# Moving row loads to the GpSimd DMA queue and cutting block stores into quarters in a serial backward chain

## The chip, the cores and the metric

The kernel runs on one core of one Trainium2 chip. The metric is the device time of one execution in microseconds (us). Times are medians of several executions. Of a kernel's stages only the backward chain is changed, so a second number is used throughout: **the chain time**, read from the trace as the time from the first to the last of the copies that close a step (`GT<-ps_sum`), 63 step intervals. Each chain time below is of a single profile, and differences below about 3 us are not read.

## The reference, cut to what matters

The output is `x` plus two branches on its layer norm, and the kernel computes it together with all gradients. The first branch is recurrent: 64 segments of 32 rows, each attending over itself and over 8 memory rows that the segment before produced.

```python
mem = mem0
for s in range(n_seg):                                   # 64 segments
    xs = x[:, s * seg_len:(s + 1) * seg_len, :]          # 32 rows of 512
    h = jnp.concatenate([mem, xs], axis=1)               # 8 memory rows + 32
    q, k, v = (jnp.einsum('btd,dhe->bhte', h, W) for W in (Wq, Wk, Wv))   # 32 heads of 128
    p = _softmax(jnp.where(mask, jnp.einsum('bhqe,bhke->bhqk', q, k) * scale, -1e9))
    o = jnp.einsum('bhte,hed->btd', jnp.einsum('bhqk,bhke->bhqe', p, v), Wo)
    mem = o[:, :M, :]                                    # read by the next segment
    outs.append(o[:, M:, :])
# second branch: out = relu(x @ w1 + b1) ** 2 @ w2 + b2
_out, _vjp = jax.vjp(_f, x, mem0, Wq, Wk, Wv, Wo, w1, b1, w2, b2)
```

(The `q, k, v` line and the softmax are shortened here.) Because a segment's memory gradient comes from the segment after it, the backward pass is a chain of 64 steps that cannot overlap.

## The kernel before

The backward chain takes its steps in blocks of four, 16 blocks. One list of names per step (`B_ORDER`) fixes the order in which operations are issued. A bare name is an operation of this step, `-` means that of the step before, `L.` one of the block before, and `L.` with `+` one of this block. Each engine executes its own instructions in that order.

```python
B_ORDER = (
    "... o1te ldq- ldn- L.qo ldk- vtr vg0 ... qeb0 ldp kg0 ... qp1 ldn ... ra L.G1 sm vc sF L.H1 sT HT",   # first step
    ...,
    "L.ra3 o0mm L.qst o0ev L.ldt+ ... s1 d11 vg0 ldk- vlb1 ... vtr L.gs+ vla1 ldq- ... vc vg1 ... qp0 L.vo+ "
    "qeb0 ... L.ldv+ kp1 ... qp1 L.ldk+ qeb1 qea1 ldp kg1 L.ko+ qg1 ra sm sF L.sT sT HT")               # last step
```

All DMAs are issued by the SP queue (`dma = nc.sync.dma_start`). Of each step these are the loads of P, qN, kN and kLs, and a DMA transpose into `vl`, which two GpSimd copies then turn into `vT`. A step's names of row loads, `vtr` and `vc` stand for those of the step that comes next. So `ldq-` and `ldk-`, and `ldn-` in two steps of four, load rows of the very step in which they are issued.

```python
def ldp():
    dma(tile_of("P", [P, KH, KW])[:], rows[:, 3 * GW:AC].rearrange("p (k n) -> p k n", k=KH))
o["ldq"] = lambda: dma(tile_of("qN", [P, GW])[:], rows[:, GW:2 * GW])
o["ldn"] = lambda: dma(tile_of("kN", [P, GW])[:], rows[:, 2 * GW:3 * GW])
o["ldk"] = lambda: dma(tile_of("kLs", [P, GW])[0:P - M * j, :], S_NL[b, M * j:P, 1, :])
def vtr():
    nc.sync.dma_start_transpose(tile_of("vl", [P, KH, HG, SEG])[:]..., rows[:, 0:GW])
def vc():
    vT = tile_of("vT", [P, KH, HG, L])
    nc.gpsimd.tensor_copy(vT[:, :, :, 0:SEG], C["vl"][:])
    nc.gpsimd.tensor_copy(vT[:, :, :, SEG:L], B_["vTL"][:, :, :, lc])
```

The gradients gv, gk and gq of a block's four steps are collected in three tiles and stored once a block, 1 MB each. Every partition's 8 KB is contiguous on both sides, so a store has 8 KB descriptors:

```python
for t, n in enumerate("qkv"):
    o[n + "o"] = lambda n=n, t=t: dma(S_GB[b, t], B_["g" + n][:].rearrange("p g k j r -> p g k (j r)"))
```

TensorE's part is made of small matmuls: `outer` (into `b_pp`, in the chain of waits below 32 instructions in some 0.3 us) and `gather` (into `ps_gR`, 16 in about 1 us).

Of the kernel before, what the change touches and what calls it, by code (L numbers as in the profile page):

```python
# [10 lines left out]
BF16 = mybir.dt.bfloat16  # L11
F32 = mybir.dt.float32
P = 128
# [13 lines left out]
def kernel(  # L27
# [27 lines left out]
    nc = tc.nc  # L55

    _, S, D = A_x.shape
    M = A_mem0.shape[1]
# [35 lines left out]
    out2flat = out_2.flatten_outer_dims()  # L94

    dma = nc.sync.dma_start

    const = ctx.enter_context(tc.tile_pool(name="const", bufs=1))
    dram = ctx.enter_context(tc.tile_pool(name="dram", bufs=1, space=bass.MemoryType.DRAM))
# [813 lines left out]
    with sb("ls", 3) as ls, sb("lo", 1) as lo_, psum("lpp", 1) as lpp, psum("lr", 4) as lr:  # L913
# [84 lines left out]


    B_ORDER = (  # L1000
        "o0mm o0ev xt- L.xt- o1mm o0fl vp0 L.lq o1ev o0te o1fl s0 vea0 veb0 o1te ldq- ldn- L.qo ldk- vtr vg0 "
        "vlb0 d10 vla0 vp1 d20 d30 s1 L.G0 veb1 L.H0 d11 vlb1 vla1 d40 vea1 d21 tu0 kp0 kea0 klb0 keb0 d31 vg1 "
        "d41 kla0 qp0 qea0 qeb0 ldp kg0 tu1 kp1 kea1 klb1 L.sx- keb1 kla1 qg0 qp1 ldn qea1 qeb1 L.ra0 kg1 qg1 "
        "ra L.G1 sm vc sF L.H1 sT HT",
        "L.ra1 o0mm ldk- o1mm o0ev vtr o0fl o0te vp0 veb0 xt- o1ev vlb0 vla0 L.ktr vea0 s0 o1fl vp1 o1te L.G2 "
        "d10 d20 veb1 s1 vlb1 d30 vg0 d40 vea1 tu0 ldq- vla1 kp0 vg1 d11 kea0 kla0 d21 klb0 keb0 d31 d41 L.vtr "
        "qp0 qeb0 ldp qea0 tu1 vc kg0 kp1 kea1 qg0 keb1 kla1 klb1 qp1 kg1 qeb1 qea1 qg1 L.H2 ra sm sF sT L.ra2 "
        "HT",
        "xt- o0mm o0ev o1mm o0fl o1ev ldn- ldq- ldk- vp0 o1fl o0te s0 vlb0 veb0 d10 vla0 vea0 d20 d30 o1te vp1 "
        "vg0 vlb1 vtr s1 L.G3 vc vla1 veb1 d40 vea1 tu0 L.vst d11 d21 kp0 klb0 kea0 keb0 kla0 d31 vg1 L.kst d41 "  # L1010
        "qp0 qeb0 qea0 tu1 kg0 kp1 kea1 keb1 qg0 kla1 klb1 qp1 L.qtr kg1 qeb1 qea1 qg1 ra L.H3 sm sF sT ldp ldn "
        "HT",
        "L.ra3 o0mm L.qst o0ev L.ldt+ o1mm xt- o0fl L.gl+ o1ev vp0 o1fl o0te vlb0 vea0 vla0 s0 veb0 o1te vp1 "
        "d10 d20 d30 veb1 s1 d11 vg0 ldk- vlb1 d40 tu0 vea1 vtr L.gs+ vla1 ldq- d21 L.sm kp0 klb0 vc vg1 keb0 "
        "d31 L.sF kea0 kla0 d41 qp0 L.vo+ qeb0 tu1 kg0 qea0 L.ldv+ kp1 qg0 keb1 kla1 klb1 kea1 qp1 L.ldk+ qeb1 "
        "qea1 ldp kg1 L.ko+ qg1 ra sm sF L.sT sT HT")
    ENGS = on_engines(
        "L.ra0 L.sF kea0 kea1 kla0 kla1 o0ev o1ev o1te qea0 qeb1 ra sF vea0 vea1 veb1 vla0 vla1 vlb1 "
        "xt",
# [1 line left out]
    with sb("bq", 1) as bq, sb("bs", 2) as bs, sb("bt", 1) as bt, psum("bpp", 1) as bpp, psum("br", 4) as br:  # L1021
# [11 lines left out]
        def block(b):  # L1033
            if b not in blk:
                shapes = {"gkL": (bs, [P, KH, HG, NL], BF16), "gvL": (bs, [P, KH, HG, NL], BF16),
                          "gqL": (bt, [P, KH, HG, NL], BF16), "PG": (bt, [P, 1, KH, KW], BF16), "GL": (bt, [P, 1, KH, KW], BF16),
                          "gOL": (bt, [P, GW], BF16), "qNL": (bt, [P, GW], BF16), "vTL": (bt, [P, KH, HG, NL], BF16),
                          "XT": (bs, [P, DC, SPB, SEG], F32), "R4": (bt, [P, D], F32), "F": (bt, [P, P], F32),
                          "gv": (bt, [P, HG, KH, SPB, SEG], BF16), "gk": (bt, [P, HG, KH, SPB, SEG], BF16),
                          "gq": (bt, [P, HG, KH, SPB, SEG], BF16)}  # L1040

                def make(n):
                    pool, shape, dt = shapes[n]
                    return pool.tile(shape, dt, name="b_" + n, tag=n)
                blk[b] = Tiles(make)
            return blk[b]

        def left(b):
            B_ = block(b)
            ps, st, o = {}, {}, {}  # L1050
            src = {"v": "gvL", "k": "gkL", "q": "gqL"}
            o["lq"] = lambda: dma(B_["gqL"][:], S_GQL[b])

            def following(f):

                return lambda: f(b - 1) if b > 0 else None
            for n, f in loads.items():
                o[n] = following(f)
            o["gs"] = lambda: dma(S_GM[:, :, b * P:(b + 1) * P], gts[b][:])
            for t, n in enumerate("qkv"):  # L1060
                o[n + "o"] = lambda n=n, t=t: dma(S_GB[b, t], B_["g" + n][:].rearrange("p g k j r -> p g k (j r)"))

            jobs = [(WT[t], src[n], k) for t, n in ((2, "v"), (1, "k"), (0, "q")) for k in range(KH)]
            for i in range(4):
                for x, nm in enumerate("GH"):
                    def G_(i=i, x=x):
                        if x == 0:
                            ps["R", i] = big("ps_RL")
                        for m, (W, n, k) in enumerate(jobs[6 * i + 3 * x:6 * i + 3 * x + 3]):
                            for g in range(HG):  # L1070
                                nc.tensor.matmul(ps["R", i][32 * g:32 * g + 32, :], lhsT=B_[n][:, k, g, :],  # L1071
                                                 rhs=W[:, g * KH + k, :], start=(x == 0 and m == 0),
                                                 stop=(x == 1 and m == 2), tile_position=(0, 32 * g))
                    o["%s%d" % (nm, i)] = G_
                if i == 0:
                    o["ra0"] = lambda: ENGS["L.ra0"](B_["R4"][:], ps["R", 0][:])
                else:
                    o["ra%d" % i] = lambda i=i: nc.vector.tensor_tensor(out=B_["R4"][:], in0=ps["R", i][:],
                                                                        in1=B_["R4"][:], op=ALU.add)
            sum_ops(o, big, lambda: B_["R4"], lambda: B_["F"], st, "L.")  # L1080
            o["xt"] = lambda: ENGS["L.xt"](B_["XT"][:, :, :, 0:M],
                                                st["sum"].rearrange("p c (j t) -> p c j t", j=SPB))

            for t, n in enumerate("qkv"):
                def nt(n=n):
                    st[n] = bs.tile([P, KH, P], BF16, name="gNat", tag="gNat")
                    nc.sync.dma_start_transpose(st[n][:], B_[src[n]][:].rearrange("p k g r -> p k (g r)"))
                o[n + "tr"] = nt
                o[n + "st"] = lambda n=n, t=t: dma(S_GL[b].rearrange("g r t c -> (g r) t c")[:, t, :],
                                                   st[n][:].rearrange("p k e -> p (k e)"))  # L1090

            o["sx"] = lambda: dma(S_XG[b], B_["XT"][:].rearrange("p c j r -> p c (j r)"))
            return o
# [8 lines left out]
                nc.gpsimd.memset(gts[b][:, :, P - SEG:P - SEG + M], 0.0)  # L1102

        def ldv(b):
            dma(block(b)["PG"][:, 0], S_PL[b])
            dma(block(b)["gOL"][:], S_GOL[b])

        def ldk(b):
            dma(block(b)["GL"][:, 0], S_GSL[b])
            dma(block(b)["qNL"][:], S_NL[b][:, 0, :])  # L1110

        def ldt(b):
            turned_rows(block(b)["vTL"][:], b, 2)
# [2 lines left out]
        def bwd(s):  # L1116
# [12 lines left out]
                return C[n]  # L1129

            def ldp():
                dma(tile_of("P", [P, KH, KW])[:], rows[:, 3 * GW:AC].rearrange("p (k n) -> p k n", k=KH))
            o["ldp"] = ldp
            o["ldq"] = lambda: dma(tile_of("qN", [P, GW])[:], rows[:, GW:2 * GW])
            o["ldn"] = lambda: dma(tile_of("kN", [P, GW])[:], rows[:, 2 * GW:3 * GW])
            o["ldk"] = lambda: dma(tile_of("kLs", [P, GW])[0:P - M * j, :], S_NL[b, M * j:P, 1, :])

            def vtr():

# [8 lines left out]
            for p in range(2):  # L1148
# [43 lines left out]
                for t, n in ((2, "v"), (1, "k"), (0, "q")):  # L1192
                    w = 32 if n == "q" else KW
                    for x, h in enumerate("ab"):
                        e = "%se%s%d" % (n, h, p)
                        o[e] = lambda n=n, p=p, w=w, x=x, e=e: ENGS[e](
                            B_["g" + n][:, 2 * x:2 * x + 2, HALF[p], j, :],
                            two_of(ps["x", n, p], x, w)[:, :, :, 0:SEG])
                        if n != "q":
                            e = "%sl%s%d" % (n, h, p)  # L1200
                            o[e] = lambda n=n, p=p, x=x, e=e: ENGS[e](
                                B_["g%sL" % n][:, HALF[p], 2 * x:2 * x + 2, lc].rearrange("p k g r -> p g k r"),
                                two_of(ps["x", n, p], x, KW)[:, :, :, SEG:L])

                    def G_(n=n, p=p, t=t):
                        if "R" not in ps:
                            ps["R"] = big("ps_gR")
                            ps["n"] = 0
                        ps["n"] += 1
                        gather(ps["R"], lambda k, g: B_["g" + n][:, g, k, j, :], WT[t], p, ps["n"] == 1,  # L1210
                               ps["n"] == 6)
                    o["%sg%d" % (n, p)] = G_
            def ra():
# [189 lines left out]
```

## Time and profile before

The time is 3290.86 us (2 executions, 3289.17 to 3292.55). The busy time of each engine in four stretches of the kernel before shows the stages. The columns are the stretch, its length, each engine's busy time with its instruction count, the granted TensorE clock, the busy share of the DMA engines and what they moved.

```profile
core 0: us, PE busy (x) PEld busy (x) DVE busy (x) ACT busy (x) POOL busy (x), PEclk, DMA share, GB/s
488.00:1425.00 937.00, 770.15 (x18868) 406.50 (x18868) 509.92 (x1588) 381.72 (x833) 51.54 (x128) 0.97 0.67 169
...
1602.00:2623.00 1021.00, 860.63 (x25194) 414.13 (x25195) 432.46 (x1338) 383.12 (x1181) 89.79 (x129) 0.96 0.68 176
2623.00:3266.00 643.00, 570.51 (x2682) 262.57 (x2733) 58.50 (x89) 74.81 (x161) 36.99 (x32) 0.95 0.97 192
```

The first row is the forward chain (recurrence forward), the second the backward chain with its start and end, the last the weight gradients. TensorE is busy 861 of 1021 us.

The steps of a block are not alike: on average 18.9, 14.1, 14.3 and 16.4 us from first to last. The middle two show what a step costs; the excess sits around a block's turn. What TensorE and then the SP queue waited for in the backward stretch of the kernel before (columns: who waited for whom, us in total, times, longest):

```profile
PE b_pp L563 <- issue: 45.8, 34, 4.7
PE ps_gR L478 <- issue: 20.8, 16, 2.8
PE ps_proj L437 <- DVE GT L424: 17.9, 63, 0.3
...
PE b_pp L563 <- DMA b_qN<-S_A: 12.3, 11, 2.7
```

```profile
SPq L1132 <- DVE gS L522: 215.1, 48, 9.8
SPq L1135 <- PE b_pp L563: 148.5, 49, 6.7
```

"Issue" means that the profile shows nothing that TensorE waited for. The wait for GT belongs to every step (0.3 us, 63 times). The wait for `b_qN` is a load that came late, and the two SP lines say why: SP stands in line, 215 us before the load of P and 149 us before that of kN, and what is behind cannot leave.

The chain of waits of the kernel before, around one block's last step (columns: start, length, what), has both kinds of gap:

```profile
2034.34 3.92 DMA b_qN<-S_A
...
2040.92 0.18 PE b_pp L563 x12
2041.10 2.77 issue
2043.88 0.32 PE b_pp L563 x12
```

First TensorE waits for a load that took 3.92 us. Then it stops for 2.77 us in the middle of a run of 32 matmuls, where the profile shows nothing that it waits for. The DMA records suggest why: an instruction fetch runs from 2041.37 to 2042.25 us, and TensorE resumes 1.6 us after it landed. In the queue part of the page of the kernel before, queue 8 holds these fetches (columns: packets, MB, share of the 16 engines' time):

```profile
q1 hardware_dynamic: 890418, 625.81, 77.0%
q8 instruction: 406, 6.65, 0.8%
```

6.65 MB in 406 fetches is 16 KB each; 192 of them fall in the chain, one per 256 instructions. I call a gap between matmuls of over 0.8 us a **fetch gap** when it ends 1.0 to 1.8 us after a fetch landed. The chain before has 34 of them, 66.1 us of its 74.7 us in gaps over 0.8 us. (The prediction counted a slightly longer window: 35, 68 us.) That they are stalls on the fetch is an inference from this timing.

### The profile page before, as it was taken

The numbers are of one execution on the slowest core, as the hardware profiler recorded it, in microseconds if no ns is written. First come the engines' busy times: TensorE is split into PE (matmuls) and PEld (weight loads), VectorE is DVE, ScalarE is ACT, GpSimd is POOL, SyncE is SP. The second block draws the span as 40 slices with busy tenths as digits, with TensorE's granted clock in tenths as the row PEclk, the third lists the DMA queues.
The fourth block names the chain that finished last, engine by engine and source line by source line (L and its number), as shares of the span: only waits on it lengthen the run. The fifth ranks groups of instructions, "written<-read, shape, count | busy, mean of one in ns | idle before, by whom it ended". The sixth has DMA issues, their size and how long they took to land.

```text
span 3266.8 us, 115469 instructions
## 1 busy us (share of the span) xinstructions
PE 2704.2 (83%) x51673; PEld 1338.9 (41%) x51768; DVE 1220.4 (37%) x3526; ACT 1017.1 (31%) x2492; POOL 193.7 (6%) x345
## 2 busy tenths in 40 slices
PE   8898778888888888834688888888888866999998
PEld 4453334444444444412344344344344423444444
DVE  4440035555655555523344344444444400010001
ACT  3331124444444444412333333333333401111111
POOL 0000000000000000000000010010000000000000
PEclk9999899999999999966799999999999988999999
DMA  9958894676667676689668666666776699999993
GB/s 254 283 145 312 293 291 114 165 179 162 185 164 184 161 184 161 171 235 256 185 164 210 166 164 181 189 164 172 190 183 172 173 260 199 205 186 224 187 187 91
DMA packets 890915, 633.20 MB, mean 194 GB/s; under 512 B 659745, under 2 KB 748466, under 8 KB 881074
## 3 DMA queue, kind: packets, MB, share of 16 engines
q1 hardware_dynamic: 890418, 625.81, 77.0%
q8 instruction: 406, 6.65, 0.8%
q14 instruction: 91, 0.75, 0.1%
HBM read 227.16 MB, written 250.10 MB: 146 GB/s over the span
## 4 chain that ended last, share of the span: by engine, by line
PE 57%; DMA 13%; SPq 13%; DVE 7%; issue 5%; ACT 5%; ACTq 0%; POOLq 0%; POOL 0%; DVEq 0%
PE ps_gR L478 11%; PE ps_proj L437 11%; PE ps_gw L1364 8%; SPq L1289 6%; PE b_pp L563 3%; PE ps_R L478 3%; DMA S_GOL<-l_gON 3%; PE ps_tr L167 2%; ACT R L421 2%; PE ps_sum L489 2%; PE ps_L L406 2%; DMA out_dram<-wt 2%; PE ps_w L366 2%; PE ps_w L386 1%; PE ps_RL L1071 1%
## 5 line engine op out<-in xcount | busy, mean ns | idle before, releaser
L1364 PE MATMUL ps_gw<-gn,HNc 128*128 128x512 bf16 x1881 | 416.5, 380 | 8.3 <-ACT wt L1339 6.3
L437 PE MATMUL ps_proj<-Wqkv,X 128*32 128x512 bf16 x6144 | 361.9, 385 | 18.2 <-DVE X L424 17.9
L1364 PEld LDWEIGHTS <-HNc 128*128 128x128 bf16 x1920 | 188.2, 98 | 231.9 <-issue 9.5
L421 ACT CAST f_N<-ps_proj 128x512 bf16<-128x512 f32 x320 | 185.4, 583 | 258.0 <-PE ps_proj L437 243.7
L1339 ACT CAST wt<-ps_gw 128x512 bf16<-128x512 f32 x126 | 69.5, 591 | 541.8 <-DMA out_dram<-wt 353.1
L437 PEld LDWEIGHTS <-X 128*32 128x32 bf16 x6144 | 156.9, 98 | 174.7 <-DVE X L424 29.9
L1322 DVE TENSOR_TENSOR gx<-ps_rows,gb 128x512 f32<-128x512 f32 x16 | 11.1, 692 | 427.5 <-PE ps_rows L1320 396.8
L1364 PE MATMUL ps_gw<-GOc,gn 128*128 128x512 bf16 x627 | 142.2, 387 | 19.2 <-DMA gn<-S_ON 18.3
L478 PE MATMUL ps_gR<-WT,b_gq 128*32 128x512 bf16 x2048 | 145.2, 401 | 7.8 <-issue 7.5
L478 PE MATMUL ps_gR<-WT,b_gk 128*32 128x512 bf16 x2048 | 145.8, 404 | 5.8 <-issue 5.7
L478 PE MATMUL ps_gR<-WT,b_gv 128*32 128x512 bf16 x2048 | 142.5, 393 | 7.6 <-issue 7.5
L437 PE MATMUL ps_proj<-WoT,GT 128*32 128x512 bf16 x2048 | 125.6, 388 | 22.5 <-DVE GT L424 17.9
L478 PE MATMUL ps_R<-Wo,OT 128*32 128x512 bf16 x2048 | 127.1, 390 | 0.0
L1145 POOL COPY b_vT<-b_vl 128x1024 bf16<-128x1024 bf16 x64 | 66.7, 1042 | 905.9 <-PE ps_sc L458 521.4
L421 ACT CAST gON<-ps_proj 128x512 bf16<-128x512 f32 x128 | 75.0, 586 | 118.9 <-PE ps_proj L437 115.2
L489 PE MATMUL ps_sum<-R,sel 128*32 128x128 f32 x1152 | 61.2, 285 | 58.4 <-ACT R L421 53.0
L1364 PEld LDWEIGHTS <-gn 128*128 128x128 bf16 x640 | 63.6, 100 | 96.4 <-DMA gn<-S_ON 18.6
L406 PE MATMUL ps_L<-Wqkv,XL 128*128 128x512 bf16 x376 | 84.8, 385 | 18.2 <-DMA XL<-S_XL 16.8
L421 ACT CAST b_gq<-b_pp 128x256 bf16<-128x256 f32 x128 | 47.7, 373 | 161.4 <-PE b_pp L563 153.3
L421 ACT CAST b_gk<-b_pp 128x256 bf16<-128x256 f32 x128 | 47.8, 373 | 150.7 <-PE b_pp L563 115.5
L424 DVE CAST b_gq<-b_pp 128x256 bf16<-128x256 f32 x128 | 54.4, 425 | 107.0 <-PE b_pp L563 102.8
L437 PEld LDWEIGHTS <-GT 128*32 128x32 bf16 x2048 | 49.5, 98 | 78.4 <-DVE GT L424 30.0
(214 smaller groups left out, 4427.9 us busy)
## 6 DMA issues: line engine op xcount, KB each, us to landing
S_A<-f_N SPq DMA_DIRECT2D x64, 512.0 KB
out_dram<-wt SPq DMA_DIRECT2D x154, 128.0 KB
S_A<-f_N SPq DMA_DIRECT2D x64, 256.0 KB
S_ON<-OC SPq DMA_DIRECT2D x64, 256.0 KB
b_qN<-S_A SPq DMA_DIRECT2D x64, 256.0 KB
b_kN<-S_A SPq DMA_DIRECT2D x64, 256.0 KB
S_GB<-b_gv SPq DMA_DIRECT2D x16, 1024.0 KB
S_GB<-b_gk SPq DMA_DIRECT2D x16, 1024.0 KB
```

What stands on the lines that cost most here:

```text
L167: nc.tensor.transpose(ps_ap, in_ap, ident[base:base + k, base:base + k])
L366: nc.tensor.matmul(ps[:], lhsT=aN[:, rc, fc * P:(fc + 1) * P], rhs=gN[:, rc, :], start=(rc == 0), stop=(rc == TC - 1))
L406: nc.tensor.matmul(ps[:], lhsT=XL[:, dc, q * P:(q + 1) * P], rhs=Wqkv[:, dc, c0:c0 + 512], start=(dc == 0), stop=(dc == DC - 1))
L421: nc.scalar.copy(out, in_)
L437: nc.tensor.matmul(ps[32 * g:32 * g + 32, :], lhsT=hT[:, dc, :], rhs=W[:, dc, c:c + 4 * P], start=(dc == 0), stop=(dc == DC - 1), tile_pos ...
L478: nc.tensor.matmul(R[32 * g:32 * g + 32, :], lhsT=XT(k, g), rhs=W[:, g * KH + k, :], start=(first and k == 4 * h), stop=(last and k == 4 * ...
L489: nc.tensor.matmul(ps["n"][SEG * c:SEG * c + SEG, 0:P], lhsT=sel[:], rhs=R4()[:, c * P:(c + 1) * P], start=True, stop=True, tile_position= ...
L563: nc.tensor.matmul(o, lhsT=N_[32 * g:32 * g + m, kk * P:(kk + 1) * P], rhs=X(kk)[32 * g:32 * g + m], start=(i == 0), stop=(i == len(jobs) ...
L1145: nc.gpsimd.tensor_copy(vT[:, :, :, 0:SEG], C["vl"][:])
L1289: nc.sync.dma_start_transpose(t_[:, b, :].rearrange("p (k e) -> p k e", k=KH), blocks(b)[:, g].rearrange("p k r -> p (k r)"))
L1339: nc.any.tensor_copy(wt[:], ps[:])
L1364: nc.tensor.matmul(ps[:], lhsT=l(rc), rhs=r(rc), start=(n == 0), stop=(n == RC_ALL - 1))
```

## The change

The intent: no load stands behind SP's waits, each arrives a step ahead, and stores are small and leave as soon as their data is there. It has three parts: row and block loads are issued by GpSimd, a step ahead; each 1 MB store becomes four of 256 KB, with 1 KB descriptors, each behind its copies; and the turned left values `vTL` get a second buffer (at the cost of one of `gNat`), so their transpose moves from the last step of the block before to its second step. `vtr` stands at the start of each step and `vc` behind the scores. (The transposes into `gNat` and their stores move a little too, all on SP.) The order of work on TensorE, VectorE and ScalarE stays.

```diff
+    pdma = nc.gpsimd.dma_start
     B_ORDER = (
-        "o0mm o0ev xt- ... ldq- ldn- L.qo ldk- vtr vg0 ... qeb0 ldp kg0 tu1 kp1 ... qp1 ldn ... ra L.G1 sm vc sF L.H1 sT HT",
+        "o0mm vtr o0ev xt- ... d30 s1 vc L.G0 ... d41 ldp kla0 ... kp1 ldq kea1 ... qp1 ldn ldk qea1 ... L.H1 sT HT",
   ... (second and third step alike)
-        "... L.ldt+ ... ldk- ... vtr ... ldq- ... vc vg1 ... qp0 L.vo+ ... L.ldv+ ... L.ldk+ ... ldp kg1 L.ko+ qg1 ..."
+        "... vtr ... vea0 L.voa0+ ... veb0 L.vob0+ o1te vp1 L.ldv+ ... veb1 L.vob1+ s1 vc ... vea1 L.voa1+ ... keb0 L.kob0+ "
+        "... kea0 L.koa0+ ... ldp qp0 qeb0 L.qob0+ ... qea0 L.qoa0+ kp1 L.ldk+ ldq ... keb1 L.kob1+ ... kea1 L.koa1+ "
+        "qp1 ldn ldk qeb1 L.qob1+ qea1 L.qoa1+ kg1 qg1 ra sm sF L.sT sT HT"
-    "vTL": (bt, [P, KH, HG, NL], BF16)      # one buffer
+    "vTL": (bs, [P, KH, HG, NL], BF16)      # two
-    "gv": (bt, [P, HG, KH, SPB, SEG], BF16), "gk": ..., "gq": ...
+    **{"g%s%d" % (n, p): (bt, [P, HG, KH // 2, SPB, SEG], BF16) for n in "qkv" for p in (0, 1)}
-    o[n + "o"] = lambda n=n, t=t: dma(S_GB[b, t], ...)
+    for p in range(2):
+        for x, h in enumerate("ab"):
+            def so(n=n, t=t, p=p, gs=slice(2 * x, 2 * x + 2)):
+                dma(S_GB[b, t][:, gs, HALF[p]], B_["g%s%d" % (n, p)][:, gs].rearrange("p g k j r -> p g k (j r)"))
+            o["%so%s%d" % (n, h, p)] = so
-    st[n] = bs.tile([P, KH, P], BF16, name="gNat", tag="gNat")
+    st[n] = bt.tile([P, KH, P], BF16, name="gNat", tag="gNat")
   ... in ldv, ldk, ldp, ldq, ldn: dma(...) becomes pdma(...)
```

## The prediction

> **What bounds the kernel.** By busy times per stretch, the backward chain takes 1025 of 3267 us (1600 to 2625), TensorE busy 863 of it, the DMA engines 68%. It is 64 steps in series. Taking the copy that closes each step (GT<-ps_sum) as a clock, the four steps of a block take on average 18.9, 14.1, 14.3 and 16.4 us (first to last): 63.6 a block. Gaps between matmuls are 3.3, 1.4, 1.4 and 3.8 us of that; about 1.2 us of each is the step's own chain (sum, turn, copy), which stays. So at most some 5 us a block, 80 us in all, can be won, in the last step of a block and the first of the next.
>
> **What the excess is.**
> 1. In the waits of this window TensorE waits for nothing visible ("issue") before b_pp 34 times, 45.8 us, and before ps_gR 16 times, 20.8 us. Of 43 matmul gaps over 0.8 us (85 us), 35 (68 us) end 1.0 to 1.8 us after an instruction fetch (queue 8, 16 KB each) has landed, nearly all with 8 KB descriptors moving in the 6 us before: the S_GB stores, 1 MB each. The forward chain, at the same DMA share (0.66), with 147 fetches but no 8 KB descriptors, has only 3 such gaps (3.5 us). So I think the fetch stands behind 8 KB descriptors (median 0.31 us each). The Trainium skill (DMA: Bandwidth & Descriptors, "Queues, rings and completion order") says that each engine takes turns between queues a whole packet at a time. An engine's share of a store is eight descriptors: I estimate up to 2.5 us in front of a fetch.
> 2. TensorE waits for b_qN 11 times, 12.3 us, nearly always in a block's last step; for b_P and b_kLs 4 us. The loads stand behind a wait in SP's queue: 215 us for gS (before b_P), 149 us for b_pp (before b_kN).
> 3. ScalarE's copies into b_gk wait for "issue" up to 5.8 us; probably for the gk store still reading.
>
> **What the change does.** TensorE, VectorE and ScalarE work stays. Loads of rows go to GpSimd, a step ahead: P, qN, kN, kLs land before the next step uses them. GpSimd's two copies take 1.4 us of a 15.8 us step; if issuing costs about 1 us for each of 5 DMAs (an assumption), it stays under half busy. The skill ("Issuing engines are not separate DMA queues") says this adds no bandwidth; I count only on the lost blocking. The stores become twelve of 256 KB with 1 KB descriptors (0.046 us each here: about 20% more engine time for the same bytes): packets in front of a fetch become 16 KB. gk and gq leave earlier.
>
> **Sum (estimates).** Fetch gaps 68 us to 10 to 20: -52. Waits for loads: -15. Copies behind stores: -4. Back: more descriptors, GpSimd's queue as a third competitor, lower granted clock with denser matmuls (0.96 now): +8. Net -63 us, all on the critical path.
>
> Predicted 3228 us; 8 in 10 between 3195 and 3265. Faster by over 2% (below 3225): 0.46; within 2%: 0.50; slower: 0.04.
>
> **Shows right or wrong.** Last and first steps of a block fall to about 14.7 and 17.0 us, the middle ones stay; 8 KB descriptors gone from the chain; fetch gaps under 20 us; no DMA wait before b_qN; SP's 215 and 149 us gone; other stages unchanged.
>
> **What would make it wrong.** GpSimd's issue costing several us, so that vT or P come late; fetches still late because 3 MB of stores crowd into one step, with a third queue; small descriptors saturating the engines; a clock that falls.

## The result, and the profile after

The kernel after takes 3298.27 us (3296.58 to 3299.97), 1.0026 times the time before, with a 95% interval of 1.0002 to 1.005: the same within 2%, and rather slower. (Ratios here and below are the mean time of one kernel's fast runs over that of the other's of the same rounds, so not quite the ratio of the medians quoted.) The predicted 3228 us was 70 us too low.

The busy time of the backward and the last stretch of the kernel after:

```profile
...
1614.00:2639.00 1025.00, 858.90 (x25191) 413.70 (x25191) 431.83 (x1338) 383.44 (x1181) 262.83 (x449) 0.96 0.72 175
2639.00:3294.00 655.00, 567.83 (x2682) 262.06 (x2733) 58.52 (x89) 74.97 (x161) 36.97 (x32) 0.94 0.93 188
```

The first row shows the same TensorE work and 4 us more time. GpSimd went from 90 to 263 us busy. The chain itself is 984.0 us (983.0 before), and its steps are 18.4, 14.5, 14.4 and 16.4 us: the first step of a block won half a microsecond, the middle ones lost a little. The unchanged last stage differs by 12 us: the profiled execution of the kernel before was a quick one, and a later one of the same kernel took 3284.5 us with the same chain (run a4).

What TensorE waited for in the backward stretch of the kernel after:

```profile
PE b_pp L564 <- issue: 63.0, 49, 3.7
PE ps_gR L479 <- issue: 23.9, 20, 3.1
PE ps_proj L438 <- DVE GT L425: 17.9, 63, 0.3
...
PE b_pp L564 <- DMA b_P<-S_A: 6.5, 1, 6.5
```

The waits for loads are gone: no line of `b_qN`, and `b_P` only once, in the very first step. (There `vc` stands in front of the load of P in GpSimd's queue and waits for its transpose; the first step takes 25.2 us instead of 20.3, which is 5 of the 7 us that the timed runs show.) But "issue" before `b_pp` and `ps_gR`, the line that the quarter stores should have emptied, grew from 66.6 to 86.9 us. Fetch gaps are 41, 74.9 us, instead of 34, 66.1 us.

The queues of the kernel after, and what SP waited for:

```profile
q1 hardware_dynamic: 890482, 556.07, 70.4%
q0 software_dynamic: 22528, 69.75, 7.7%
q8 instruction: 406, 6.65, 0.9%
```

```profile
SPq L1145 <- POOL b_vT L1151: 202.0, 42, 11.0
SPq L1064 <- ACT b_gvL L422: 164.0, 19, 19.4
```

Queue 0 is GpSimd's, with 70 MB of loads. SP's old waits of 215 and 149 us are gone as predicted; but SP still stands 202 us, now for the GpSimd copy that frees `vl` (L1145 is the transpose into it), and 164 us before the block's stores (L1064). All lines of this view, summed over the chain, are 603 us, against 500 before: SP does not stand less, it stands in front of other DMAs. It no longer waits at a load in the middle of the step, and the transpose leaves the moment that copy is done. The GpSimd work in the backward stretch of the kernel after, costliest groups (columns: line, engine, operation, tiles, shapes, count, busy us, mean ns, idle time before):

```profile
L1150 POOL COPY b_vT<-b_vl 128x1024 bf16<-128x1024 bf16 x64 | 66.9, 1045 | 406.7 <-issue 204.8 <-PE ps_sc L459 97.9 <-DMA b_vl<-S_A 82.7
L1141 POOL DMA_DIRECT2D b_kLs<-S_NL x64 | 35.3, 552 | 4.9 <-PE ps_gR L479 2.6 <-PE b_pp L564 2.1
...
L1140 POOL DMA_DIRECT2D b_kN<-S_A x64 | 34.4, 538 | 63.8 <-PE b_pp L564 63.8
```

Issuing one load costs GpSimd 0.54 to 0.55 us (538 and 552 ns in the lines shown), half of what the prediction assumed, and GpSimd is busy a quarter of the time. So the first way in which the prediction expected to fail is not what happened.

One stall of the chain of waits after, this time in the middle of a run of 16 `gather` matmuls (start, length, what):

```profile
1693.32 0.30 PE b_pp L564 x32
1693.61 0.33 PE ps_gR L479 x4
1693.94 1.84 issue
1695.79 0.83 PE ps_gR L479 x12
```

The DMA view of the stretch 1687 to 1697 us of the kernel after, in 40 slices of 0.25 us (busy tenths of the DMA engines, and GB/s), with what was issued in it:

```profile
DMA  9999999999999892450599999990000059999989
GB/s 389 389 381 377 373 381 373 387 384 349 306 239 175 144 109 81 67 42 23 92 286 389 271 246 366 267 244 0 0 7 10 9 115 295 276 292 285 290 172 196
...
b_vl<-S_A SPq DMA_TRANSPOSE x2
b_vTL<-S_NL SPq DMA_TRANSPOSE x1
gNat<-b_gkL SPq DMA_TRANSPOSE x1
```

The block's first step began at 1687.06. Up to 1690.75 the engines are full, at first with 370 to 390 GB/s, and from 1689.5 on with 306, falling to 109 GB/s, although just as full: the transposes, whose pieces are 256 bytes. They are full again from 1692.0 to 1693.75. In that time, at 1693.24, the fetch that TensorE wants begins; it lands at 1694.28, and TensorE, stopped since 1693.94, resumes at 1695.79, 1.5 us later. (A fetch occupies one of 16 engines, too little for these digits.) The records don't show when a fetch was asked for, so how long it waited is not seen directly; that full engines hold it back is inferred from where the gaps fall, below.

### The profile page after: what moved, and what is told of

Same layout as the page of the kernel before. It is cut to its first block, busy times and chain, and to the rows that moved or that the text cites. A ratio compares the mean times of both kernels' runs of the same rounds, so it can differ in the third digit from the quotient of the medians.

```text
span 3294.7 us, 115991 instructions
## 1 busy us (share of the span) xinstructions
PE 2700.7 (82%) x51673; PEld 1338.1 (41%) x51768; DVE 1220.0 (37%) x3526; ACT 1017.3 (31%) x2492; POOL 366.7 (11%) x665
## 3 DMA queue, kind: packets, MB, share of 16 engines
q0 software_dynamic: 22528, 69.75, 7.7%
q8 instruction: 406, 6.65, 0.9%
## 4 chain that ended last, share of the span: by engine, by line
PE 60%; DMA 12%; SPq 10%; DVE 7%; ACT 6%; issue 5%; ACTq 0%; POOL 0%; POOLq 0%; DVEq 0%
PE ps_proj L438 12%; PE ps_gR L479 12%; PE ps_gw L1369 9%; SPq L1294 5%; PE b_pp L564 4%; PE ps_R L479 3%; PE ps_tr L168 2%; ACT R L422 2%; DMA S_GOL<-l_gON 2%; PE ps_sum L490 2%; PE ps_RL L1076 2%; PE ps_w L367 2%; PE ps_w L387 1%; PE ps_B L311 1%; PE ps_sum L498 1%
## 5 line engine op out<-in xcount | busy, mean ns | idle before, releaser
L810 POOL COPY kM<-f_kT 128x256 bf16<-128x256 bf16 x64 | 25.8, 403 | 831.9 <-ACT f_kT L422 644.3
```

## The experiments

Three theories of where the gain went.

- **T1, GpSimd's queue.** The quarter stores do what was hoped, but loads in GpSimd's software queue, a third competitor for the DMA engines, delay fetches.
- **T2, timing.** SP, which used to stand before loads in the middle of each step, now reaches its transposes earlier, and they meet the stores in the stretch where TensorE uses up instructions fastest.
- **T3, full engines alone.** Small descriptors never helped, because full engines, not large packets, delay the fetch.

The recorded expectations use names of their time: T1 in them is the prediction's view (8 KB descriptors delay the fetch), T2 there is T3 here, M is T2 here, and T1b and Q are T1 here. A, B, A1 and A2 are explained where they occur.

In the table every kernel is given with its chain; the texts follow run by run. The steps are the mean of a block's first to last. Fetch gaps are count and us in the chain, and half clock is the time in the chain at half of the full clock; a field is empty where it was not read.

| run | edit | median us | ratio to before (95%) | chain us | steps us | fetch gaps | half clock us |
|---|---|---|---|---|---|---|---|
| before | | 3290.86 | | 983.0 | 18.9 14.1 14.3 16.4 | 34, 66 | 65 |
| after | | 3298.27 | 1.0026 (1.0002 to 1.005) | 984.0 | 18.4 14.5 14.4 16.4 | 41, 75 | 55 |
| a1 | after, loads on SP | 3260.27 | 0.9917 (0.9867 to 0.9968) | 954.4 | 17.0 14.5 14.4 15.9 | 26, 41 | 41 |
| a2 | before, quarter stores | 3262.95 | 0.9921 (0.9873 to 0.9969) | 959.8 | 17.5 14.3 14.2 16.0 | 21, 31 | 41 |
| a3 | after, no stores | 3260.74 | 0.9914 (0.9883 to 0.9944) | 925.3 | 16.2 14.4 14.3 14.9 | 24, 33 | 17 |
| a4 | before again, one look | 3284.52 | | 983.6 | 19.0 14.2 14.3 16.2 | 28, 58 | 68 |
| b1 | a3, loads on SP, one look | 3231.26 | | 914.9 | 15.6 14.4 14.4 14.7 | 16, 19 | 0 |
| b2 | after, loads on ScalarE's queue | 3359.03 | 1.0174 (1.0128 to 1.022) | 1051.2 | 18.3 15.0 15.1 19.6 | 17, 23 | |
| b3 | after, only P and qN on GpSimd, one look | 3269.70 | | 956.4 | 16.8 14.3 14.3 16.5 | 28, 47 | 38 |
| b4 | a1, late stores moved to the next block | 3259.75 | 0.9887 (0.9853 to 0.9921) | 947.4 | 17.0 14.2 14.4 15.7 | 26, 37 | 31 |
| c1 | after, `vc` later | 3275.17 | 0.9989 (0.9956 to 1.0022) | 962.3 | 17.6 14.0 14.3 16.4 | 29, 54 | 65 |
| c2 | c1, b4's stores, P first at the start | 3262.13 | 0.9958 (0.9937 to 0.9979) | 960.1 | 17.4 14.1 14.2 16.4 | 34, 58 | |
| c3 | a1, k and q stores behind the loads | 3234.58 | 0.9871 (0.9853 to 0.989) | 937.7 | 16.5 14.0 14.2 15.9 | 23, 34 | 31 |
| d1 | a1, transposes early | 3265.13 | 0.9934 (0.9902 to 0.9965) | 966.7 | 17.5 14.6 14.6 15.7 | 30, 43 | 38 |
| d2 | c3, v stores too | 3261.59 | 0.9927 (0.9894 to 0.9961) | 961.4 | 18.7 14.3 14.4 14.7 | 16, 20 | |
| d3 | c3, P and qN on GpSimd | 3256.59 | 0.9904 (0.9868 to 0.994) | 956.4 | 16.8 14.3 14.3 16.5 | 26, 39 | |
| d4 | after again, one look | 3300.02 | | 986.1 | 18.6 14.5 14.4 16.3 | 41, 71 | 75 |
| e1 | after, SP made to stand | 3280.89 | 0.9985 (0.9961 to 1.0009) | 971.4 | 17.0 14.3 14.4 17.2 | 32, 55 | |
| e2 | c1, loads on SP | 3255.37 | 0.9898 (0.9867 to 0.9928) | 947.8 | 16.8 14.4 14.2 15.9 | 23, 37 | 34 |

Runs of one letter shared a chip. All kernels but a3 and b1 gave the right result. By the 2% rule every timed version is the same as the kernel before, but b2, which is unclear; what is read below is the chain. Repeats show how well the other columns hold: fetch gaps 66 and 58 us, 75 and 71; half clock 65 and 68 us, 55 and 75.

Most expectations were missed in number. Expected fetch gaps against measured, in us: a1 under 25 or 55 to 90, 41; a2 under 25 or 50 to 90, 31; a3 under 15, 33 (its chain, 50 to 70 shorter, was met); b1 under 12 or 25 to 40, 19; b2 30 to 50 or 65 to 85, 23; b3 50 to 60, 47; b4 25, 37; c1 40 or 65 to 85, 54; c2 35, 58; c3 20 to 30, 34; d1 55 to 75, 43; e1 40 to 50 or over 65, 55. e2 met its second case (948 us, near 40). Where two theories stood against each other, the result mostly lay between them.

### Which part won and which lost: a1 to a4

a1 is the kernel after with the loads back on SP, at their new places:

```diff
-    pdma = nc.gpsimd.dma_start
+    pdma = nc.sync.dma_start
```

> The changed kernel with its row loads issued on SP again, in the changed order; everything else as changed. Theory T1b (the 8 KB descriptors did block the instruction fetch, but the third queue now does it instead): matmul gaps that follow an instruction fetch fall from about 70 us to under 25 us in the backward chain, though waits for loads come back. Theory T2 (any backlog that saturates the 16 engines delays the fetch, whatever the descriptor size and the number of queues): fetch gaps stay at 55 to 90 us, and the time is 3285 to 3320 us.

a2 is the kernel before with nothing but half tiles and quarter stores, at the places of the old stores:

```diff
-  "... ldq- ldn- L.qo ldk- vtr ..."
+  "... ldq- ldn- L.qoa0 L.qob0 L.qoa1 L.qob1 ldk- vtr ..."
-  "... qp0 L.vo+ qeb0 ... ldp kg1 L.ko+ qg1 ..."
+  "... qp0 L.voa0+ L.vob0+ L.voa1+ L.vob1+ qeb0 ... ldp kg1 L.koa0+ L.kob0+ L.koa1+ L.kob1+ qg1 ..."
```

> The kernel before with only its three 1 MB stores of a block cut into quarters (1 KB descriptors), at the places where the whole stores stood; loads stay on SP. Theory T1 (8 KB descriptors stand in front of the fetch): fetch gaps fall from 68 to under 25 us, time about 3240 us. Theory T2 (saturation): fetch gaps stay at 50 to 90 us, time 3280 to 3310 us.

a3 is the kernel after without its stores, except for one block, which the last stage then reads 16 times. Three gradients are wrong, and only its chain can be compared:

```diff
-    dma(S_GB[b, t][:, gs, HALF[p]], ...)
+    if b == NB - 1:
+        dma(S_GB[b, t][:, gs, HALF[p]], ...)
-    got[i] = rows_of(g, lambda b: S_GB[b, t], ...)
+    got[i] = rows_of(g, lambda b: S_GB[NB - 1, t], ...)
```

> The changed kernel with the S_GB stores of 15 of 16 blocks left out (wrong results on purpose in three weight gradients; the last stage reads the one stored block 16 times, so its own traffic is unchanged). Theory T2: without the 3 MB per block the engines are not saturated, fetch gaps fall under 15 us, first and last steps of a block fall to about 15.5 and 14.5 us, the chain gets 50 to 70 us shorter: time about 3240 us. Theory T1b (third queue): most fetch gaps stay, less than 25 us gained.

a4 is the kernel before, unchanged, for a second profile.

> The kernel before once more, for a second profile: how much the length of each stage varies from run to run. I expect the backward chain within 5 us of 983 us (63 steps), and other stages to vary by up to 10 us, as those of the changed kernel did though nothing in them changed.

What was measured is plain. The quarter stores alone win 23 us of the chain (983 to 960), and their fetch gaps are half as long (31 us for 66 and 58). T3 falls: small packets do help, though not down to the 10 to 20 us predicted. The TensorE waits of a2 in the chain:

```profile
PE b_pp L563 <- issue: 25.3, 36, 2.6
...
PE ps_gR L478 <- issue: 13.7, 18, 2.2
...
PE b_pp L563 <- DMA b_qN<-S_A: 12.1, 9, 2.7
```

"Issue" fell from 66.6 to 39.0 us, and the wait for `b_qN` stays, since the loads stayed. And the kernel after with its loads on SP (a1) is 30 us quicker in the chain than with them on GpSimd. So **one line of the change, the queue of the loads, gave back all that the rest had won.** a1's wait lines in a stretch around the chain (TensorE, then SP):

```profile
PE b_pp L564 <- issue: 41.2, 45, 2.9
...
PE ps_gR L479 <- issue: 18.7, 22, 2.1
```

```profile
SPq L1137 <- DVE gS L523: 185.0, 48, 7.5
```

"Issue" is 59.9 us instead of 86.9 us, and there is no wait for `b_qN` either: to load a step ahead was enough, and needed no other queue. Note the SP line: with the loads back, SP stands 185 us at the load of P. Without its stores (a3) the kernel after needs 925 us, so 59 us of its chain hang on their traffic.

### Is it GpSimd's queue, or any second queue? b1 to b4

b1 is a3 with a1's line. b2 and b3 are the kernel after with other queues, and b4 is a1 with the last stores of a block (half of gk and all of gq) moved into the next block's first step.

> The run without S_GB stores once more, but with the row loads on SP (wrong results on purpose in three weight gradients). With the loads on GpSimd 24 fetch gaps, 33 us, were left although the stores were gone. Theory A (it is the loads' own queue that holds the fetch up): fetch gaps fall under 12 us. Theory B (any traffic of this kind leaves such gaps; the queue is no matter): they stay at 25 to 40 us.

```diff
-    pdma = nc.gpsimd.dma_start      # b2
+    pdma = nc.scalar.dma_start
```

> The changed kernel with the row loads on ScalarE's hardware queue in place of GpSimd's software queue. Theory A1 (a third queue of any kind takes turns from the fetch): fetch gaps near those of the GpSimd version, 65 to 85 us. Theory A2 (it is GpSimd's software descriptors): fetch gaps near those of the SP version, 30 to 50 us. In both, ScalarE stands in order before its loads, so that part of the time may be lost there; the fetch gaps are the measure, not the time.

```diff
-    o["ldn"] = lambda: pdma(...)    # b3; also ldk and the block loads
+    o["ldn"] = lambda: dma(...)
```

> The changed kernel with only P and qN of each step on GpSimd; kN, kLs and the loads per block on SP. If the gaps come from the bytes that the software queue moves (about 40% of those of the changed kernel stay there), fetch gaps lie between 41 us (all on SP) and 75 us (all on GpSimd), about 50 to 60, and the 63 steps between 954 and 984 us, about 965.

```diff
-  "o0mm vtr ... L.xt- o1mm o0fl vp0 ... o1fl s0 ... s1 vc ..."      # b4, loads on SP
+  "o0mm vtr ... L.xt- o1mm L.kob1 L.koa1 o0fl vp0 ... o1fl L.qob0 L.qoa0 s0 ... s1 L.qob1 L.qoa1 vc ..."
```

> An attempt to beat both: the changed kernel with row loads on SP, and half of the k quarters and all q quarters of a block's stores moved from its last step into the first step of the next block. If the fetch gaps come from the length of the saturated stretch, spreading the stores lowers them from 41 to about 25 us and the chain from 954 to about 940 us, time ratio to before about 0.987. If instead the stores now collide with the next block's copies, the chain gets no shorter than 954.

Without stores, the loads' queue is worth 10 us (925 to 915), a third of what it is worth with them (30). The cost therefore comes mostly from the meeting of the two, as both theories would have it. With P and qN alone on GpSimd (b3) the chain is 956 us, almost a1's. So here two of a step's four loads on that queue cost nothing that can be read, and all of them 30 us. (d3 below found otherwise.)

b2 decides little, though I had hoped it would. ScalarE issues its DMAs in the order of its copies and stands at their waits, so it becomes a bottleneck itself (b2, TensorE waits in the chain):

```profile
PE b_pp L564 <- ACT b_gk L422: 41.9, 15, 4.7
```

Its fetch gaps are few (23 us), but a slower chain also asks for instructions more slowly.

### Timing: c1, d1, e1, and c2, e2

c1 leaves the loads on GpSimd and moves only GpSimd's copies behind the step's loads, so that `vl` comes free later and SP's next transpose cannot run ahead:

```diff
-  "... d30 s1 vc L.G0 ... ldp kla0 ... kp1 ldq kea1 ... qp1 ldn ldk qea1 ..."
+  "... d30 s1 L.G0 ... ldp kla0 ... kp1 ldq kea1 ... qp1 ldn ldk vc qea1 ..."   # all four steps
-  "L.ra1 L.ldt+ o0mm L.ktr vtr o1mm ..."
+  "L.ra1 o0mm L.ktr vtr L.ldt+ o1mm ..."
```

> The changed kernel, loads still on GpSimd; only GpSimd's copy of the turned values into vT moves from the middle to the end of a step (after the last load), so that SP's next turn (the DMA transpose into vl, which waits for that copy) can start only near the end of the step; the turn of vTL is put behind it. Theory M (timing: with no loads in its line SP never stands, so the turns of 256 B pieces come right behind the stores, into the stretch of the block's first step where TensorE uses up instructions fastest): fetch gaps fall from 75 to about 40 us and the 63 steps from 984 to about 950 us, as with loads on SP. Theory Q (GpSimd's queue itself, as a third one that takes turns, delays the fetch): fetch gaps stay at 65 to 85 us, the chain at 975 to 990 us.

The chain falls from 984 to 962 us, two thirds of what the loads' queue had cost. TensorE's waits in c1:

```profile
PE b_pp L564 <- issue: 44.2, 36, 2.9
PE ps_gR L479 <- issue: 18.1, 18, 3.1
```

That is 62.3 us of "issue", close to a1's 59.9, although its fetch gaps as counted, 54 us, are more than a1's 41. (c1 also lets GpSimd's loads leave before its copies, so it isn't SP's timing alone that moves. In the timed runs it wins less: 12 us over the kernel after, give or take 13.) A likely mechanism is seen in what the DMA engines do at the turn of a block. From the DMA records I summed the time that the 16 engines spent, in bins of 2 us from the start of a block's first step, as a mean over the blocks (not a view of the profile; sums go slightly over 1 where the records of packets overlap):

```
us from the turn        -8    -6    -4    -2     0     2     4     6     8    10    12    14
before  all           0.79  0.49  0.82  0.98  1.00  1.02  1.04  0.88  0.44  0.25  0.19  0.23
        256 B pieces  0.00  0.00  0.00  0.00  0.00  0.06  0.29  0.63  0.33  0.00  0.00  0.00
        fetch gaps us  2.8  12.8   1.1   0.0   0.0   0.0   1.1   5.3  11.6  17.5   0.0   0.0
after   all           0.98  0.95  0.94  1.02  1.04  1.12  1.21  1.15  1.14  1.02  0.77  0.71
        256 B pieces  0.12  0.09  0.01  0.00  0.04  0.36  0.84  0.74  1.03  0.86  0.40  0.21
        fetch gaps us 14.1  11.4   3.1   0.0   0.0   0.0   0.0   8.6  12.9   6.9   9.5   0.0
a1      all           0.94  1.00  0.94  0.90  0.99  1.00  1.08  0.87  0.49  0.25  0.54  0.77
        256 B pieces  0.09  0.15  0.01  0.00  0.03  0.13  0.55  0.64  0.19  0.00  0.00  0.09
        fetch gaps us  6.8  10.1   0.8   0.0   0.0   0.0   2.1   0.8  10.0   5.8   0.0   0.0
c1      256 B pieces                                0.42  0.77  0.63  0.47  0.24  0.00  0.03
```

In the kernel after, the engines stay full until 12 us into the first step; in a1 they have room from 8 us on. The difference is the 256-byte pieces, the transposes: at 8 to 12 us they take the whole of the engines' time in the kernel after and almost none in a1. In the middle steps of the kernel before TensorE starts 55 to 100 instructions per us (weight loads counted) between 2 and 11 us of a step, and 10 to 45 at its start and end. When a fetch begins, never more than some 280 instructions are left in front of it (counted from the driest moment of the trace), some 4 us at that pace. Engines that are just as full outside this stretch make no gaps: the kernel before has 1.04 and 1.11 at 18 to 22 us, with none. Its own gaps mostly end at 8 to 12 us, when the engines have room again; but the fetches behind them began with the engines full (1.05 to 1.22 over the 4 us before).

d1 is the reverse of c1: loads on SP, but the transpose issued early, right behind the copy that frees its tile, as SP does it in the kernel after.

```diff
-  "o0mm vtr o0ev ... d30 s1 vc L.G0 ..."        # a1, all four steps alike
+  "o0mm o0ev ... d30 s1 vc vtr+ L.G0 ..."
```

> The changed kernel with loads on SP (a1: 954 us for 63 steps, fetch gaps 41 us), but the next step's DMA transpose put right behind GpSimd's copy, ahead of the loads in SP's line, so that it starts in the middle of a step, as it did in the changed kernel. Theory M (timing of the transposes): fetch gaps rise to 55 to 75 us and the chain to 968 to 985 us though all loads are on SP. Theory Q (GpSimd's queue): both stay at 41 and 954 us.

This costs 12 us of chain (954 to 967), so early transposes are harmful without GpSimd's queue too, as far as one profile shows (the timed runs differ by 6 us, give or take 20). My expectation for the fetch gaps was missed (43 us, hardly more than a1's 41): the loss spread over shorter gaps.

e1 leaves every load on GpSimd and makes SP stand, by two stores of 64 bytes per step that nobody reads. One needs gS and one gq1, about where SP used to wait:

```diff
+  o["w1"] = lambda: dma(S_W[s, 0:1, :], gS[0:1, 0, 0:SEG])              # behind ldp
+  o["w2"] = lambda: dma(S_W[s, 1:2, :], B_["gq1"][0:1, 0, 0, j, :])     # behind qg1
```

> The changed kernel, all loads on GpSimd, with two 64-byte stores per step added on SP (of gS behind d41, of gq at the step's end), only so that SP stands in its line where it stood for the loads of P and kLs. Theory M (timing): although 128 DMAs are added, the chain gets shorter, to 950 to 962 us, fetch gaps 40 to 50 us. Theory Q (queue): chain 975 us or more, fetch gaps 65 us or more. In between: both have a share, in proportion.

The chain falls by 13 us (984 to 971), and e1's SP wait in it says how much SP stands:

```profile
SPq L1145 <- DVE b_gq L426: 239.4, 48, 8.5
```

Two useless DMAs a step make the kernel quicker, by 1.0026 to 0.9985 in the ratios. That is the clearest evidence for T2. The gain lies where T2 puts it: a block's first step falls from 18.4 to 17.0 us, as in a1. Its last step grows from 16.4 to 17.2, probably because SP now stands before the block's stores as well. SP's waits in the chain sum to 565 us, less than the 603 of the kernel after: what counts is not how long SP stands, but before which DMA. e1 and c1 do not win all 30 us. e2 asks what remains: c1's order, with loads on SP.

```diff
-    pdma = nc.gpsimd.dma_start
+    pdma = nc.sync.dma_start          # in c1
```

> c1's order (vT copied at the end of a step) with the loads on SP. Theory M: the same as c1 within 8 us (962; fetch gaps 54 us), since both turn late. If GpSimd's queue costs of itself: shorter than c1 by 10 us or more, about 948 us, fetch gaps near 40 us.

947.8 us, against c1's 962.3. In one and the same order the queue is worth 14 us (in the timed runs 30, give or take 15). So T1 has a share too. c2, which adds b4's store places to c1, asks whether stores can win the rest; it also loads P before the first `vc`:

```diff
-  "... qeb0 L.qob0+ ... qea0 L.qoa0+ ... keb1 L.kob1+ ... kea1 L.koa1+ ... L.qob1+ ... L.qoa1+ kg1 ..."
+  "... qeb0 ... qea0 ... keb1 ... kea1 ... kg1 ..."                    # moved to the next block's first step, as in b4
-  for n in ("vtr", "vc", "ldp", "ldq", "ldn", "ldk"):
+  for n in ("vtr", "ldp", "vc", "ldq", "ldn", "ldk"):
```

> The same with the stores spread as in the attempt b4 (k half, q all into the next block's first step), and at the start P loaded before the first vT copy. Theory M: fetch gaps about 35 us, chain about 945 us, first step back from 25 to 20 us; ratio to before about 0.988. Theory Q: as changed kernel, 975 to 990 us.

The chain is 960 us, no better than c1's within what can be read. The very first step fell from 24.8 to 21.0 us, which confirms why the kernel after starts slowly.

### A version that beats both: c3, and what spoils it, d2 and d3

c3 is a1 with the k and q stores taken out of the last step's busy part. Half of gk goes after the loads at its end, and the rest after the transpose at the start of the next block; gv stays behind its copies.

```diff
-  "o0mm vtr o0ev ..."                                                        # first step
+  "o0mm vtr L.kob1 L.koa1 L.qob0 L.qoa0 L.qob1 L.qoa1 o0ev ..."
-  "... keb0 L.kob0+ ... kea0 L.koa0+ ... L.qob0+ ... qp1 ldn ldk qeb1 L.qob1+ qea1 L.qoa1+ kg1 ..."   # last step
+  "... keb0 ... kea0 ... qp1 ldn ldk L.kob0+ L.koa0+ qeb1 qea1 kg1 ..."
```

> Loads on SP, and all k and q quarters issued behind the last load of the block's last step, so that they run in the stretch in which TensorE uses up few instructions (end of a step and first 2 us of the next). If the gap needs both a saturated ring and a hungry stretch, the gaps of the last step (17 us of 37 in b4) go, those of the first step stay or grow a little: fetch gaps 20 to 30 us, chain about 940 us. If stores then run into the first step's copies, ScalarE waits for S_GB and the chain stays at 947 or above.

It takes 3234.58 us (3229.85 to 3239.09), 0.9871 of the kernel before, and is the best of all correct kernels. By the 2% rule it is still the same as the kernel before, but its interval lies wholly below 1. TensorE's waits in its chain:

```profile
PE b_pp L564 <- issue: 27.7, 29, 2.3
...
PE ps_gR L479 <- issue: 16.8, 22, 2.6
```

"Issue" is 44.5 us, against 66.6 before and 86.9 after.

d2 moves the v stores behind the loads as well:

```diff
-  "... vea0 L.voa0+ ... veb0 L.vob0+ ... veb1 L.vob1+ ... vea1 L.voa1+ ... ldn ldk L.kob0+ L.koa0+ ..."
+  "... vea0 ... veb0 ... veb1 ... vea1 ... ldn ldk L.vob0+ L.voa0+ L.vob1+ L.voa1+ L.kob0+ L.koa0+ ..."
```

> c3 with the four v quarters moved, too, behind the last load of the block's last step, so that no store runs in that step's hungry stretch. The gaps of the last step (18 us in c3) should go; but 3 MB now leave at the turn of the block, and the copies of the next first step into v may have to wait for their stores: if ScalarE then waits for S_GB by more than 15 us in all, the chain is no shorter than c3's 938 us; otherwise about 925 us.

It has the fewest fetch gaps of all correct kernels (20 us) and yet a chain of 961 us. The stores are now so late that the next block's copies meet tiles that are still being read (d2, ScalarE's wait, then TensorE's behind it, in the chain):

```profile
ACT b_gq L422 <- DMA S_GB<-b_gq: 50.5, 15, 4.3
```

```profile
PE b_pp L564 <- ACT b_gq L422: 25.0, 14, 3.1
...
PE ps_gR L479 <- ACT b_gv L422: 5.6, 9, 1.0
```

These 25.0 and 5.6 us, less the 7 us by which "issue" fell (44.5 to 37.7), make up the 24 us lost. A layout with two buffers of the stored tiles might remove this wait; no run tries it.

d3 is c3 with P and qN on GpSimd, as b3 was a1 with them there; c2's start is included.

```diff
-    pdma = nc.sync.dma_start
+    pdma = nc.gpsimd.dma_start        # in c3; kN, kLs and the block loads stay on SP
```

> c3 with P and qN of each step on GpSimd (kN, kLs and the loads per block stay on SP and keep it standing until the end of the step). b3 against a1 showed no loss from this (956 against 954 us), so I expect the same time as c3: 930 to 945 us for the chain, ratio to before 0.985 to 0.990.

The chain is 956 us instead of 938, where I had expected 930 to 945. The same two loads cost 19 us here (11 in the timed runs, give or take 14), though in a1's order they cost 2. d4 is the kernel after, again:

> The changed kernel once more, for a second profile: chain within 5 us of 984 us, fetch gaps 65 to 85 us, first step about 25 us.

Its chain, 986.1 us, is within 2 us of the first.

### What is settled and what is open

Settled by runs: the quarter stores win 23 us of chain; loading a step ahead ends the waits for `b_qN`; the move of the loads to GpSimd costs 30 us of chain; part of that is timing, since e1 moves the timing alone, and c1 and d1 little else.

Not settled: the split. c1 puts timing at 22 us, e1 at 13, d1 at 12; the queue in one and the same order costs 14 us (c1 and e2), 10 (a3 and b1), 19 (c3 and d3) or 2 (a1 and b3). As estimates from these, timing is 12 to 22 of the 30 us, and the queue most of the rest. The timed ratios agree in sign, but with intervals of about ±0.3%, 10 us, they cannot split 30 us; taken as they are, they would give the queue the larger share (c1 wins 12 us, e1 13, and from c1 to e2 it is 30). In what way the queue itself costs is open. I had thought of its packets standing in front of the fetches. The records do not support it: queue 0 has 0.15 of the engines' time in the 4 us before stalled fetches and 0.23 before all fetches. All queues together have 1.04 before stalled ones (kernel before), against 0.66 on the mean of all. Full engines go with stalls; the software queue's share of them doesn't. Nor do full engines explain every stall: without the stores all queues have only 0.56 (a3) and 0.60 (b1) in those 4 us.

One rival was not tested. The loads also travel in larger packets on GpSimd's queue. The same 69.75 MB are, in the page of b2 on ScalarE's queue and above in that of the kernel after on GpSimd's (q0: 22528):

```profile
q10 hardware_dynamic: 45248, 69.75, 7.6%
```

By the DMA records GpSimd's queue moves nearly all of it in packets of 4 KB (159 ns each), the other in packets of 1 and 2 KB (46 and 84 ns). So the move made for the loads the opposite of what the quarters made for the stores. Whether an engine has to finish such a packet before it turns to a fetch, and whether that costs anything here, no run shows.

## Why the prediction was wrong, point by point

- **What bounds the kernel: right.** The excess lies only in a block's last and first step, and the middle steps moved by little more than half a us at most in any kernel with loads on SP or GpSimd. The gaps after fetches were the right suspects.
- **"Fetch gaps 68 us to 10 to 20: -52": the first term that failed.** The mechanism was right in kind: the small stores, alone, halve the gaps (58 to 66 down to 31 us). The size was off by half: 27 to 35 us were won, not 48 to 58. Large packets were at most one way of making a fetch late: a1, without one 8 KB descriptor in its chain, keeps 41 us, most of them behind full engines (0.98 in the 4 us before), and 3 MB of stores crowd into one step as before. The prediction named this among its failures ("fetches still late because 3 MB of stores crowd into one step, with a third queue"). In the whole change the gaps were 75 us. The forward chain, which the prediction took as its control, was not an equal one: TensorE issues 40 instructions per us there (37,736 in 937 us), against 49.
- **"Waits for loads: -15": right in mechanism.** The 12.3 us for `b_qN` went to nothing, and a1 kept that without GpSimd. Their end is in a1's gain, but what it is worth alone was not run.
- **"Copies behind stores: -4": not shown.** No run takes it alone. d2 shows that the opposite exists: stores left too late cost 25 us.
- **"Back: ... +8": the term that decided it.** It was to hold more descriptors, the third queue and a lower clock. The queue of the loads alone cost 30 us of chain, and the start 5. I had looked at SP's 364 us of standing as waste. It was also what kept most of SP's transposes away from the turn of a block: at 8 to 12 us of its first step their 256-byte pieces take a third of the engines' time or none before, and nearly all of it after. "I count only on the lost blocking": by c1 and e1, 13 to 22 us of the loss came from just that.
- **"GpSimd's issue costing several us": didn't happen.** It costs 0.54 us.
- **A lower clock "with denser matmuls": the wrong sign.** The half clock follows gaps. Of 202 half-clock stretches (3.4 us or a multiple) in the chains of all nineteen profiles, 170 begin within 1.5 us of a gap over 0.8 us; of all moments of a chain some 15% lie so near to one. Half-clock time in the chain falls with the gaps, if roughly: 65 us before, 55 after (75 in d4), 41 in a1 and a2, 31 in c3, none in b1. What this adds to a gap's cost was not measured by itself; over the chains of all profiles but b2's, 1 us of gaps over 0.8 us goes with 1.1 us of chain. The Trainium skill (TensorE: Matmul & The Clock Gate, "Part 1: The HAM clock gate") says that the gate falls back to half rate after about one idle window of 3.4 us; the windows' length agrees here, but far shorter gaps precede them.
- **Signs that were to be seen.** 8 KB descriptors are gone from the chain (5760 before, none after): right. SP's two waits gone: right, and misleading. First and last steps at 17.0 and 14.7: measured 18.4 and 16.4, while a1 has 17.0 and 15.9. Other stages unchanged: right within their own spread.

With the gain as a1 has it, 29 us of chain, the time would have been about 3260, within the range. So most of the miss lies in two terms: the fetch gaps, of which only half could be had, and one line of the diff, the loads' queue, whose cost I had booked under +8.

## What to carry to other kernels

A queue that stands in line is also a clock: before taking its waits away, ask what it will issue early, and into which stretch of the busy engine's work. Look for what seem stalls on instruction fetch where a dense run of small matmuls meets full DMA engines (gaps in mid-run that end a fixed time after a fetch landed); cut large stores that run there, and keep transposes of small pieces out of it. To load a step ahead on the same queue gave what the second queue promised, and cost less.

## What the Trainium skill lacked or had wrong

- "DMA: Bandwidth & Descriptors", section "Issuing engines are not separate DMA queues", says that issuing from several engines only saves the sequencer's time. The move from SP to GpSimd changed the chain by 30 us, and by 14 us in one and the same order (962.3 and 947.8 us). This section lacks that the choice also changes when everything else in both queues is issued, and the size of the packets (22,528 against 45,248 for the same bytes).
- "Runtime: NRT & Kernel Launch", section "Instruction fetch mechanics", calls the crossing of a 16 KB block mostly hidden. Blocks of 16 KB agree with the trace (406 fetches, 6.65 MB), but 34 of the 192 in this chain showed, at 66 us (41 and 75 us after), mostly where full DMA engines met TensorE's dense stretches (55 to 100 instructions per us). The section gives TensorE room for 2048 instructions and, further on, speaks of only two lines of 16 KB. Here a fetch never began with more than some 280 instructions left in front of it, which fits two lines of 256 rather than the 2048.
- The same page "DMA: Bandwidth & Descriptors", section "Queues, rings and completion order", says that an engine switches between queues a whole packet at a time. The halved gaps of the quarter stores alone (66 and 58 us to 31) agree with it, without proving it. How long a fetch waits for its turn when several queues are full, no run here shows: the records do not tell when it was asked for.
- "TensorE: Matmul & The Clock Gate", section "Part 1: The HAM clock gate", warns of idle gaps of about 3.4 us. Here 170 of 202 half-clock stretches began within 1.5 us of a gap of over 0.8 us, most of these gaps (85%) shorter than 3 us.
- No page that I found says how long GpSimd itself is busy with issuing one plain load of this size: 0.54 to 0.55 us here, for 128 to 256 KB.
